# First V products and early gathers of a BigBird attention feeding a mixture of experts: who writes which half of the columns, and in what order the queues run

## The chip, the cores and the metric

One core of one Trainium2 chip runs the whole program: four batches of block-sparse attention, then a dropless mixture of experts on the attention's output. The metric is the device time of one execution in microseconds (us), as the median of several executions of the same program. The kernel before takes 633.23 us (three runs, 632.06 to 638.4).

## The reference, cut to what matters

```python
# attention: B, H, S, D = 4, 8, 768, 64; blocks of 32 rows, 24 of them
scores = scale * q @ k.T
mask = |block_i - block_j| <= 1, or either is the first or last block,
       or block_j is one of 3 sampled blocks of block_i
attn = exp(scores, masked) / (sum + 1e-9)
x = (attn @ v) as rows of B*S = 3072 tokens by H*D = 512
# mixture of experts: 8 experts, F = 1024
logits = x @ w_gate; e = argmax; gate = softmax(logits)[e]
y = gate * (relu(x @ w1[e]) @ w2[e])
```

All of it is float32. The first and the last 32 queries of a batch see every key; every other query sees a few blocks.

## The kernel before, in words

**Steps.** Attention runs in 48 steps, twelve to a batch: six groups of 128 queries, the last group first (`order`, line 98), and each group in two halves (`half` 0 and 1) of two head pairs. Steps are numbered 0 to 47 here; a batch's steps are 0 to 11, 12 to 23, 24 to 35, 36 to 47. The group that comes first in each batch (GL = 5) differs: 64 of its queries are ordinary, and the other 64 are the batch's first and last 32 rows, which see all 768 keys.

**Software pipeline.** In step i TensorE makes the scores of step i (`scores_near`, `scores_drawn`; `scores_all`, `scores_two` for the first group), ScalarE makes their exponentials (line 322), VectorE multiplies by the mask (lines 361, 396), and then TensorE makes the V products of step i - 1 (`attend`, `attend_last`; the matmul is line 416). VectorE divides them by their sums (`divide`, lines 483 to 489) and SP stores the rows in HBM (line 495). In batch 0 the products of the 64 queries that see all keys are made before step 0 for all four head pairs (`attend_all`, called in a loop behind `scores_first`).

**Column halves.** A V product is 128 keys by 64 queries times 128 by 65: it uses 64 of TensorE's 128 columns. `product` (line 412) writes rows 0 to 63 of a PSUM bank for `ti` 0 and rows 64 to 127 for `ti` 1. In the ordinary groups `ti` alternates from one product to the next. In the first group the ordinary 64 queries are `ti` 0 and the 64 that see all keys are `ti` 1: six products against twelve for each head pair, so six of the twelve stand alone, and in batch 0 all are made one half after the other.

**What feeds a step.** K and Q of the next batch come as eight pieces (n = 0 to 7: even K, odd Q, one for each head pair); SP loads each by two DMAs of 192 KB in 256-byte runs (`fill_stage`, line 143), and in steps 2, 4, 6 and 8 of a batch TensorE transposes two pieces (`turn`, line 181). V of the next batch is loaded and written out as rows of 2080 bytes (lines 164, 173). For a group's sampled blocks GpSimd gathers V rows by four indirect DMAs (`fetch_values`, line 568): (ti, ch) = (0,0), (1,0), (0,1), (1,1); products of the first chunk need neither, of the second chunk ch 0, of the third ch 1. A one-element copy (`not_before`, line 582) holds GpSimd's queue until a named piece of work is done. Keys of sampled blocks are copied by VectorE and ScalarE (`place_keys`, line 627), queries by VectorE (`place_queries`, line 609).

**Queues.** The order on TensorE, VectorE, GpSimd, ScalarE and SP is as the program is written. SP's queue holds the loads of K, Q and V, the stores of V rows and of the attention's rows, and in the last batch the expert weights: whatever waits there holds up all behind it. Pieces of the routing's layout (`early`, mostly VectorE) stand in half-0 steps.

**After attention** TensorE takes tiles of tokens through two layers (lines 1199 and 1213), with weights streamed ahead; the first tiles' rows are gathered (line 1117) in steps 45 to 47.

Of the kernel before, what the change touches and what calls it, by code (L numbers as in the profile page):

```python
# [17 lines left out]
def kernel(  # L18
# [367 lines left out]
    def scores_two(b, half):  # L386

        s, par = scored(), parity(b, GL)
        for i in range(2):
            pr = 2 * half + i  # L390
            to = s[:, i, : 6 * D].rearrange("p (h c q) -> p h c q", h=2, c=3)
            for ch, keys in enumerate([xk[:, par, pr, :]] + [kr[:, par, 0, pr, P * j : P * (j + 1)] for j in range(2)]):
                chunk_products(to[:, :, ch, :], keys, qz[:, pr, 0])
        e = exps(s, 6 * P * (3 * half + 2), 6 * D)
        both = e.rearrange("p i (h c q) -> p (i h) c q", h=2, c=3)
        nc.vector.tensor_tensor(both, both, mask[:, GL, :, 0, :].unsqueeze(1).to_broadcast([P, 4, 3, D]), op=ALU.mult)

        def at(i, hh, ch):
            x = (3 * hh + ch) * D
            return e[:, i, x : x + D]  # L400

        return at, e
# [9 lines left out]

    def product(b, g, pr, ti, hh, e, values, last):
        bank, begun = bank_of(b, g, pr)
        op = bank[:, : 4 * (D + 4)].rearrange("p (r h w) -> p r h w", r=2, h=2)
        nc.tensor.matmul(  # L416
            op[ti * D : (ti + 1) * D, pr % 2, hh, : D + 1], lhsT=e, rhs=values[:, (2 * pr + hh) * VW : (2 * pr + hh + 1) * VW],
            start=ti not in begun, stop=last, skip_group_check=True,
        )
        begun.add(ti)  # L420
# [9 lines left out]
    def attend_all(b, pr, e, chunks):  # L430
        for c in chunks:
            for hh in range(2):
                product(b, GL, pr, 1, hh, e(hh, c), sets[b][2][:, c, :], c == NCH - 1)

    def attend_last(b, pr, e_all, e_two):
        for ch in range(3):
            for hh in range(2):
                product(b, GL, pr, 0, hh, e_two(pr % 2, hh, ch), values_of(b, GL, 0, ch), ch == 2)
                if e_all is not None:
                    product(b, GL, pr, 1, hh, e_all(hh, ch), sets[b][2][:, ch, :], False)  # L440
        if e_all is not None:
            attend_all(b, pr, e_all, range(3, NCH))
# [29 lines left out]
    for pr in range(NPR):  # L472
        attend_all(0, pr, es[pr], range(NCH))
# [5 lines left out]
    def divide(b, g, half):  # L479
# [13 lines left out]
        if half == 1:  # L493
            for p, n, row in pieces(g):
                nc.sync.dma_start(x_d[b * S + row : b * S + row + n, :DM], xb[p : p + n, :])
# [31 lines left out]
    def logits(b, g, beside=None):  # L527
# [5 lines left out]
        for c in range(DB):  # L533
            for j in range(2):
                nc.tensor.matmul(
                    lg[j * D : (j + 1) * D, :], lhsT=xo[:, c * P + j * D : c * P + (j + 1) * D], rhs=wg[:, c, :],
# [848 lines left out]
    for i, (b, g, half) in enumerate(steps):  # L1385
# [15 lines left out]
        if two:  # L1401
# [4 lines left out]
            fetch_values(b_, g_, 0, 1)  # L1406
        if half == 1 and i + 1 < len(steps):
            place_queries(*steps[i + 1][:2], 0)
# [26 lines left out]
        if half == 1 and i + 1 < len(steps):  # L1435
            not_before(e[0:1, 0, 0:1])
            fetch_values(*steps[i + 1][:2], int(two), 1)
# [13 lines left out]
        if i > 0 and before[0][1] != GL:  # L1451
            attend(before)
        elif i > 0:
            for b_, g_, pr, e_all, at in before:
                attend_last(b_, pr, e_all, at)
# [6 lines left out]
        if i > 0:  # L1462
            divide(*steps[i - 1])
        early(late)
        if half == 0 and nxt is not None:
# [3 lines left out]
            if i >= 2 and len(tiles_of(nxt[1])) > 1:  # L1469
                b_, g_, half_ = steps[i - 1]  # L1470
                not_before(sums[0:1, b_ * NG + g_, 4 * half_ : 4 * half_ + 1])
                fetch_values(*nxt[:2], 1, 0)
        if half == 1 and nxt is not None:
# [189 lines left out]
```

## Time and profile before

| what | us |
|---|---|
| median of three runs | 633.23 (632.06 to 638.4) |
| the profiled execution, its own time | 632.67 |
| its span, first to last instruction | 631.0 |
| TensorE matmuls busy | 603.7 |
| VectorE, ScalarE, GpSimd busy | 329.6, 231.3, 188.1 |
| last V product of attention starts | 274.2 |

The page of the profile gives for each engine the busy time; the timeline gives merged instructions in order of time with the idle time before them and what ended it; the windows give busy time, granted TensorE clock (1.00 is full speed) and DMA load in a stretch. A float32 matmul stands in the trace as two records, so 48 products are 96 records. Matmul records overlap: how fast they follow each other is read from starts, not from their length. SPq and POOLq are the issuing sequencers.

### The profile page before, as it was taken

What the parts mean: (1) busy time and instruction counts of PE and PEld (TensorE: products, weight loads), DVE (VectorE), ACT (ScalarE), POOL (GpSimd) and SP (SyncE); (2) the same over time, 40 slices, a digit from 0 to 9 for tenths busy, and PEclk for the clock granted to TensorE, in tenths of its full rate; (3) what the DMA queues carried; (4) which work ended last, traced back from release to release, by engine and by line L of the source; (5) the groups of instructions that cost most, each with busy time, mean ns of one, the idle gap of its engine ahead of it and who ended that gap; (6) DMA issues with size and microseconds to landing.
All of it is one profiled execution on the core that took longest, in us unless ns stands there. A gap on an engine that the chain in (4) does not pass through costs nothing. (4 is left out here: it accounts for less than half of the span.)

```text
span 631.0 us, 19698 instructions
## 1 busy us (share of the span) xinstructions
PE 603.7 (96%) x8038; PEld 516.1 (82%) x8038; DVE 329.6 (52%) x1134; ACT 231.3 (37%) x447; POOL 188.1 (30%) x267
## 2 busy tenths in 40 slices
PE   6989999999998999999999999999999999999994
PEld 6888989998988998987777776877977787967862
DVE  7558876885688759726952494303190208203300
ACT  6457756775775668621111011111111111111110
POOL 2247853553355437610111211011401140020110
PEclk9879999999999999999999999999999999999998
DMA  8899977986895658799989999779998999779710
GB/s 267 209 183 256 249 197 181 247 234 168 180 220 178 206 161 262 270 334 378 324 305 328 341 391 344 274 251 377 397 400 304 370 398 399 270 228 407 284 41 20
DMA packets 125060, 170.83 MB, mean 271 GB/s; under 512 B 71236, under 2 KB 71237, under 8 KB 124934
## 3 DMA queue, kind: packets, MB, share of 16 engines
q1 hardware_dynamic: 114896, 137.61, 67.1%
q0 software_dynamic: 10000, 31.59, 15.9%
q8 instruction: 73, 1.20, 0.8%
q14 instruction: 53, 0.43, 0.2%
q10 hardware_dynamic: 38, 0.00, 0.0%
HBM read 150.11 MB, written 19.33 MB: 269 GB/s over the span
## 5 line engine op out<-in xcount | busy, mean ns | idle before, releaser
L568 POOL DMA_INDIRECT around<-v_rows,rows_of x88 | 103.4, 1175 | 94.8 <-PE op L416 45.6
L322 ACT ACTIVATE ea<-s 128x1024 f32<-128x1024 f32 (+1 forms) x84 | 81.3, 969 | 58.3 <-PE s L332 41.4
L1180 DVE STREAM_TRANSPOSE around<-xg 32x128 f32<-32x128 f32 x192 | 58.1, 303 | 84.9 <-DMA xg<-x_rows,gB 79.9
L1199 PEld LDWEIGHTS hp<-around,room 128*128 128x128 f32 x832 | 94.5, 192 | 2.9 <-issue 2.7
L1199 PE MATMUL hp<-around,room 128*128 128x128 f32 x832 | 96.2, 276 | 0.0
L332 PE MATMUL s<-room,kr 128*64 128x128 f32 x1408 | 91.3, 279 | 2.7 <-DVE room L609 2.7
L416 PE MATMUL op<-around,ea 128*64 128x65 f32 x2112 | 82.9, 223 | 10.2 <-DMA around<-v_rows,rows_of 9.3
L416 PEld LDWEIGHTS op<-around,ea 128*64 128x64 f32 x2112 | 78.4, 138 | 12.6 <-DMA around<-v_rows,rows_of 10.8
L332 PEld LDWEIGHTS s<-room,kr 128*64 128x64 f32 x1408 | 80.2, 139 | 5.1 <-ACT xo L512 2.8
L1213 PE MATMUL zp<-room,kr 128*128 128x512 f32 x176 | 77.6, 594 | 0.0
L1206 ACT ACTIVATE kr<-hp 128x512 f32<-128x512 f32 x36 | 21.5, 597 | 114.4 <-PE hp L1199 103.4
L1213 PEld LDWEIGHTS zp<-room,kr 128*128 128x128 f32 x176 | 32.6, 190 | 37.2 <-issue 37.0
L1233 POOL DMA_INDIRECT out_dram<-kr,sB x14 | 14.1, 1006 | 159.1 <-ACT kr L1223 98.0
L361 DVE TENSOR_TENSOR ea<-ea,mask 128x1024 f32<-128x1024 f32 x40 | 49.3, 1234 | 11.9 <-ACT ea L322 11.0
L1199 PEld LDWEIGHTS hp<-around,other 128*128 128x128 f32 x384 | 43.8, 192 | 2.3 <-issue 2.3
L1199 PE MATMUL hp<-around,other 128*128 128x128 f32 x384 | 44.3, 275 | 0.0
L1311 DVE STREAM_TRANSPOSE ea<-ea 32x128 f32<-32x128 f32 x84 | 21.7, 285 | 31.2 <-DMA ea<-x_rows,gB 30.6
L1223 ACT ACTIVATE kr<-zp,xg 128x512 f32<-128x512 f32 x12 | 8.2, 688 | 75.7 <-PE zp L1213 75.7
L1213 PE MATMUL zp<-other,kr 128*128 128x512 f32 x80 | 35.3, 594 | 0.0
L1180 DVE STREAM_TRANSPOSE around<-kr 32x128 f32<-32x128 f32 x48 | 14.5, 303 | 36.7 <-DMA kr<-x_rows,gB 35.3
L1213 PEld LDWEIGHTS zp<-other,kr 128*128 128x128 f32 x80 | 14.9, 190 | 17.4 <-issue 17.4
L1233 POOL DMA_INDIRECT out_dram<-kr,sA x5 | 5.1, 1021 | 73.5 <-ACT kr L1223 73.5
(380 smaller groups left out, 839.0 us busy)
## 6 DMA issues: line engine op xcount, KB each, us to landing
room<-in_moe_w_dram SPq DMA_DIRECT2D x30, 2048.0 KB
other<-in_moe_w_dram SPq DMA_DIRECT2D x16, 2048.0 KB
room<-in_moe_w_dram SPq DMA_DIRECT2D x16, 512.0 KB
x_rows<-xb SPq DMA_DIRECT2D x20, 256.0 KB
room<-in_k_dram SPq DMA_DIRECT2D x24, 192.0 KB
room<-in_q_dram SPq DMA_DIRECT2D x24, 192.0 KB
v_rows<-room SPq DMA_DIRECT2D x12, 260.0 KB
v_rows<-other SPq DMA_DIRECT2D x12, 260.0 KB
```

What stands on the lines that cost most here:

```text
L322: nc.scalar.activation(e, s[:, :, :n], AF.Exp, scale=scale)
L332: nc.tensor.matmul(to[j * D : (j + 1) * D], lhsT=keys[:, j * D : (j + 1) * D], rhs=queries, start=True, stop=True)
L361: nc.vector.tensor_tensor(both, both, m[:, None, :].to_broadcast([P, 4, 4 * D]), op=ALU.mult)
L416: nc.tensor.matmul(op[ti * D : (ti + 1) * D, pr % 2, hh, : D + 1], lhsT=e, rhs=values[:, (2 * pr + hh) * VW : (2 * pr + hh + 1) * VW], sta ...
L568: nc.gpsimd.indirect_dma_start(out=around[p0:, par, 1 + ti + 2 * ch, :], out_offset=None, in_=v_d[b][:, :], in_offset=bass.IndirectOffsetO ...
L1180: nc.vector.transpose(xT[d, :, t], xg[t, :DM].rearrange("p (c q) -> p c q", c=DB)[:, :, d])
L1199: nc.tensor.matmul(hp[:, m, :], lhsT=st[i]["w1"][:, c, fb * P : (fb + 1) * P], rhs=st[i]["xT"][:, c, :], start=(c == 0), stop=(c == DB - 1),)
L1206: nc.scalar.activation(hT[:, g * (FB // 2) : (g + 1) * (FB // 2), :], hp[:], AF.Relu)
L1213: nc.tensor.matmul(zp[:], lhsT=st[i]["hT"][:, fb, :], rhs=st[i]["w2"][:, fb, :], start=(fb == 0), stop=(fb == FB - 1),)
L1223: nc.scalar.activation(zo, zp[:], AF.Copy, scale=of_i)
L1233: ins = nc.gpsimd.indirect_dma_start(out=to[:, :], out_offset=bass.IndirectOffsetOnAxis(ap=at, axis=0), in_=rows, in_offset=None, bounds_c ...
L1311: nc.vector.transpose(xT_u[d, :, j * P + tq * 32 : j * P + (tq + 1) * 32], xg_u[t, j, :DM].rearrange("p (c q) -> p c q", c=DB)[:, :, d],)
```

## The change

It has four parts, all in the attention.

1. **Column halves.** A new `side_of` gives, for the first group only, the opposite halves to the odd head pairs: the all-keys products of pair 0 write rows 64 to 127, those of pair 1 rows 0 to 63. `in_turns` issues products of the two sides alternately: in batch 0 the all-keys products of pairs 0 and 1, then 2 and 3; in the other batches all-keys products first and the ordinary ones behind them. Since odd pairs' rows now lie swapped, the first group's store is six DMAs in 512-byte runs instead of three in 2048-byte runs, and `logits` takes the swapped half.
2. **First V products of batch 0.** The ordinary products of step 0 move from step 1 into step 2, beside those of step 1; their divisions follow there. Batch 0's exponentials in `scores_two` go to other places of the buffer (`half + 4`).
3. **Gathers and queries' copies.** `place_queries` for the next group's first half moves from the start of a half-1 step to the end of the half-0 step before it, directly behind `divide`. The gather (0,1) follows it there, held by a `not_before` on those queries; (1,1) moves up to the start of the half-1 step, behind the `not_before` on the copied keys; the `not_before` on the masked exponentials is gone.
4. **Layout pieces** (`early`) come one step later, in half-1 steps, behind the gathers' issue.

```diff
-        e = exps(s, 6 * P * (3 * half + 2), 6 * D)
+        e = exps(s, 6 * P * (3 * half + 2 if b > 0 else half + 4), 6 * D)
...
+    def side_of(g, pr, ti):
+        return (ti + pr) % 2 if g == GL else ti
+
     def product(b, g, pr, ti, hh, e, values, last):
         bank, begun = bank_of(b, g, pr)
+        side = side_of(g, pr, ti)
...
-            op[ti * D : (ti + 1) * D, pr % 2, hh, : D + 1], lhsT=e, rhs=values[:, (2 * pr + hh) * VW : (2 * pr + hh + 1) * VW],
-            start=ti not in begun, stop=last, skip_group_check=True,
+            op[side * D : (side + 1) * D, pr % 2, hh, : D + 1], lhsT=e, rhs=values[:, (2 * pr + hh) * VW : (2 * pr + hh + 1) * VW],
+            start=side not in begun, stop=last, skip_group_check=True,
...
+    def of_all(b, pr, e):
+        return [(b, GL, pr, 1, hh, e(hh, c), sets[b][2][:, c, :], c == NCH - 1) for c in range(NCH) for hh in range(2)]
+
+    def of_last(b, pr, e):
+        return [(b, GL, pr, 0, hh, e(pr % 2, hh, ch), values_of(b, GL, 0, ch), ch == 2) for ch in range(3) for hh in range(2)]
+
+    def in_turns(*sides):
+        for two in zip(*sides, strict=True):
+            for one in two:
+                product(*one)
+
+    def attend_first(prs):
+        in_turns(*(of_all(0, pr, es[pr]) for pr in prs))
+
+    def attend_last(units_):
+        sides = [[], []]
+        for b, _, pr, e_all, _ in units_:
+            if e_all is not None:
+                sides[1 - pr % 2] += of_all(b, pr, e_all)
+        for b, _, pr, _, at in units_:
+            sides[pr % 2] += of_last(b, pr, at)
+        in_turns(*sides)
...
-    for pr in range(NPR):
-        attend_all(0, pr, es[pr], range(NCH))
+    for half in range(2):
+        attend_first((2 * half, 2 * half + 1))
...
+                for a in range(2):
+                    for p, n, row in pieces(g):
+                        p = (p + a * D) % P
+                        nc.sync.dma_start(
+                            x_d[b * S + row : b * S + row + n, :DM].rearrange("n (r a w) -> n r a w", r=2, a=2)[:, :, a],
+                            xb[p : p + n, :].rearrange("n (r a w) -> n r a w", r=2, a=2)[:, :, a],
+                        )
...
             if i == 1:
                 fetch_values(b_, g_, 1, 0)
-            fetch_values(b_, g_, 0, 1)
-        if half == 1 and i + 1 < len(steps):
-            place_queries(*steps[i + 1][:2], 0)
+            fetch_values(b_, g_, 1, 1)
...
-        if half == 1 and i + 1 < len(steps):
-            not_before(e[0:1, 0, 0:1])
-            fetch_values(*steps[i + 1][:2], int(two), 1)
...
-        if i > 0 and before[0][1] != GL:
+        if i == 1:
+            begun = before
+        elif i > 0 and before[0][1] != GL:
             attend(before)
         elif i > 0:
-            for b_, g_, pr, e_all, at in before:
-                attend_last(b_, pr, e_all, at)
+            for units in ([begun] if i == 2 else []) + [before]:
+                attend_last(units)
...
-        if i > 0:
+        if i == 2:
+            divide(*steps[0])
+        if i > 1:
             divide(*steps[i - 1])
-        early(late)
...
                 fetch_values(*nxt[:2], 1, 0)
+            place_queries(*nxt[:2], 0)
+            not_before(qz[0:1, 0, 0, 0, 0:1])
+            fetch_values(*nxt[:2], 0, 1)
+        early(late - 1)
```

How it moves the instructions, at three places. Names: `op` is the products' bank, `s` the scores, `tp` transposed K and Q, `xk` and `kr` keys, `around` gathered V rows, `ea` the exponentials, `room` and `other` the two big buffers that hold K, Q and V (`room` also the copied queries).

First, TensorE in batch 0, from the end of step 1's scores (first row) through steps 2 and 3. Before:

```order
L332 MATMUL s<-room,kr 64x2x64 x4
L416 MATMUL op<-around,ea 64x65 x12
L181 MATMUL tp<-ident,room 128x64 x24
L340 MATMUL s<-room,xk 128x128 x8
L332 MATMUL s<-room,kr 64x2x64 x16
L416 MATMUL op<-around,ea 64x65 x12
L332 MATMUL s<-room,kr 64x2x64 x16
L416 MATMUL op<-around,ea 64x65 x24
```

With the change:

```order
L332 MATMUL s<-room,kr 64x2x64 x4
L181 MATMUL tp<-ident,room 128x64 x24
L340 MATMUL s<-room,xk 128x128 x8
L332 MATMUL s<-room,kr 64x2x64 x16
L420 MATMUL op<-around,ea 64x65 x24
L332 MATMUL s<-room,kr 64x2x64 x16
L420 MATMUL op<-around,ea 64x65 x24
```

The twelve ordinary products of step 0 no longer stand between the scores of step 1 and step 2's transposes of K and Q pieces 0 and 1; those follow the scores at once, and the twelve stand with step 1's twelve.

Second, GpSimd through steps 4 and 5: the four gathers for step 6's group, in the order (0,0), (1,0), (0,1), (1,1), with the one-element copies that hold the queue and pieces of the routing's constants between. Before:

```order
L568 DMA around<-v_rows,rows_of 64x520
L582 COPY paced<-sums 1x1
L568 DMA around<-v_rows,rows_of 64x520
L753 IOTA kx_i 1x31
L755 CAST kx<-kx_i 1x31
L753 IOTA eid_i 1x8
L755 CAST eid<-eid_i 1x8
L582 COPY paced<-kr 1x1
L568 DMA around<-v_rows,rows_of 128x520
L582 COPY paced<-ea 1x1
L568 DMA around<-v_rows,rows_of 128x520
```

With the change:

```order
L591 DMA around<-v_rows,rows_of 64x520
L605 COPY paced<-sums 1x1
L591 DMA around<-v_rows,rows_of 64x520
L605 COPY paced<-room 1x1
L591 DMA around<-v_rows,rows_of 128x520
L776 IOTA kx_i 1x31
L778 CAST kx<-kx_i 1x31
L776 IOTA eid_i 1x8
L778 CAST eid<-eid_i 1x8
L605 COPY paced<-kr 1x1
L591 DMA around<-v_rows,rows_of 128x520
```

The third gather moves ahead of the constants and of the wait for keys (it waits for the queries now, `paced<-room`), and the fourth takes over that wait and loses the one for the exponentials.

Third, VectorE from the division in step 32. Before, the layout piece (`offA` to `slA`) follows it; behind that come, in step 33, the copied keys, and only then the queries of step 34 (line 609) and the mask of step 33:

```order
L483 TENSOR_SCALAR sums<-op 128x4
L485 RECIPROCAL r<-sums 128x4
L489 TENSOR_TENSOR xb<-op,r 128x256
L918 SCALAR_TENSOR_TENSOR offA<-loA,cnA 128x8
L919 TENSOR_SCALAR offA<-offA 128x8
L878 TENSOR_TENSOR slot<-rA,offA 128x96
L884 TENSOR_TENSOR slot<-slot,selA 128x96
L885 TENSOR_REDUCE slA<-slot 128x12
```

With the change the queries (line 632) follow that division at once, ahead of the copied keys, which begin with the load of their indices:

```order
L496 TENSOR_SCALAR sums<-op 128x4
L498 RECIPROCAL r<-sums 128x4
L502 TENSOR_TENSOR xb<-op,r 128x256
L632 COPY room<-room 64x4x64 x2
L645 TENSOR_LOAD from_k
```

and the layout piece stands behind the mask and the division of step 33:

```order
L361 TENSOR_TENSOR ea<-ea,mask 128x1024
L496 TENSOR_SCALAR sums<-op 128x4
L498 RECIPROCAL r<-sums 128x4
L502 TENSOR_TENSOR xb<-op,r 128x256
L941 SCALAR_TENSOR_TENSOR offA<-loA,cnA 128x8
L942 TENSOR_SCALAR offA<-offA 128x8
L901 TENSOR_TENSOR slot<-rA,offA 128x96
L907 TENSOR_TENSOR slot<-slot,selA 128x96
L908 TENSOR_REDUCE slA<-slot 128x12
```

So the queries have moved ahead of the layout piece and the keys, and the piece has moved back by a step.

On SP the first group's six stores (32 or 64 rows by 2 by 128) stand where three stood, in steps 2, 14, 26 and 38, ahead of the next loads of V and of K and Q pieces.

More of the change, by code (lines that the diff above doesn't have):

```diff
@@ L411, in bank_of @@
         return banks_of[key]
+    def side_of(g, pr, ti):
+        return (ti + pr) % 2 if g == GL else ti
     def product(b, g, pr, ti, hh, e, values, last):
         bank, begun = bank_of(b, g, pr)
+        side = side_of(g, pr, ti)
         op = bank[:, : 4 * (D + 4)].rearrange("p (r h w) -> p r h w", r=2, h=2)
         nc.tensor.matmul(
-            op[ti * D : (ti + 1) * D, pr % 2, hh, : D + 1], lhsT=e, rhs=values[:, (2 * pr + hh) * VW : (2 * pr + hh + 1) * VW],
-            start=ti not in begun, stop=last, skip_group_check=True,
+            op[side * D : (side + 1) * D, pr % 2, hh, : D + 1], lhsT=e, rhs=values[:, (2 * pr + hh) * VW : (2 * pr + hh + 1) * VW],
+            start=side not in begun, stop=last, skip_group_check=True,
         )
-        begun.add(ti)
+        begun.add(side)
     def attend(units_):
@@ L428, in attend @@
                         product(b, g, pr, ti, hh, e(pr % 2, hh, ti, ch), values_of(b, g, ti, ch), ch == 2)
[L430 to L442, printed above, removed]
+    def of_all(b, pr, e):
[16 more added lines that the diff above has]
+        in_turns(*sides)
     def turn_first(pr):
@@ L493, in divide @@
         if half == 1:
-            for p, n, row in pieces(g):
-                nc.sync.dma_start(x_d[b * S + row : b * S + row + n, :DM], xb[p : p + n, :])
+            if g < GL:
+                for p, n, row in pieces(g):
+                    nc.sync.dma_start(x_d[b * S + row : b * S + row + n, :DM], xb[p : p + n, :])
+            else:
+                for a in range(2):
+                    for p, n, row in pieces(g):
+                        p = (p + a * D) % P
[3 more added lines that the diff above has]
+                        )
     def pieces(g):
@@ L534, in logits @@
             for j in range(2):
+                from_ = side_of(g, c, j)
                 nc.tensor.matmul(
-                    lg[j * D : (j + 1) * D, :], lhsT=xo[:, c * P + j * D : c * P + (j + 1) * D], rhs=wg[:, c, :],
+                    lg[j * D : (j + 1) * D, :], lhsT=xo[:, c * P + from_ * D : c * P + (from_ + 1) * D], rhs=wg[:, c, :],
                     start=(c == 0), stop=(c == DB - 1), skip_group_check=True,
```

## The prediction

> **What bounds the kernel now.** I read the page first, then TensorE's waits, then windows, then the timelines of TensorE, SP, GpSimd and VectorE around each wait.
>
> ```profile
> PE 603.7 (96%) x8038; PEld 516.1 (82%) x8038; DVE 329.6 (52%) x1134; ACT 231.3 (37%) x447; POOL 188.1 (30%) x267
> ```
>
> ```profile
> PE op L416 <- DMA around<-v_rows,rows_of: 9.3, 11, 1.9
> PE s L332 <- DVE room L609: 2.7, 3, 1.7
> PE op L416 <- DVE ea L396: 0.7, 1, 0.7
> ```
>
> ```profile
> 32.50:39.30 6.80, 6.09 (x64) 5.75 (x66) 3.38 (x12) 2.14 (x5) 2.40 (x4) 0.50 1.20 234
> 39.30:203.10 163.80, 155.55 (x3652) 151.20 (x3649) 124.94 (x426) 111.49 (x212) 87.56 (x135) 1.00 0.84 207
> 203.20:206.50 3.30, 3.30 (x34) 3.30 (x34) 3.14 (x10) 0.00 (x0) 3.13 (x3) 0.50 0.89 277
> 300.00:631.00 331.00, 322.21 (x2094) 247.03 (x2093) 115.83 (x397) 48.13 (x90) 51.15 (x52) 0.99 0.84 307
> ```
>
> TensorE bounds it: 603.7 of 631.0 us. Second rows: in the attention it waits 9.3 us for gathers, 2.7 us for copied queries, 0.7 us for a mask. Windows (TensorE busy first, then loads, VectorE, ScalarE, GpSimd, clock, DMA load): the clock falls to 0.50 after two of these waits, and half speed over 6.8 and 3.4 us is 3.4 and 1.7 us lost. From 39.3 on the other engines keep TensorE over 94% busy. The experts behind 300 us are untouched.
>
> **Part 1, first V products and step 2.** Two products on the same columns follow each other; two on opposite halves share a slot.
>
> ```profile
> 20.34 2.72 PE L416 MATMUL op<-room,ea 128*64 128x65 f32 x26
> 23.23 4.12 PE L416 MATMUL op<-room,ea 128*64 128x65 f32 x67 [0.17 <-issue]
> 30.85 0.45 PE L416 MATMUL op<-around,ea 128*64 128x65 f32 x4 [0.70 <-DVE ea L396]
> 33.21 2.43 PE L416 MATMUL op<-around,ea 128*64 128x65 f32 x20 [1.91 <-DMA around<-v_rows,rows_of]
> 35.57 1.55 PE L181 MATMUL tp<-ident,room 64*128 64x64 f32 x24
> 40.86 1.50 PE L416 MATMUL op<-around,ea 128*64 128x65 f32 x23
> 43.95 1.62 PE L416 MATMUL op<-around,ea 128*64 128x65 f32 x48
> ```
>
> Single: 67 records in 4.12 us, less the last one's 0.22, are 58 ns each. Alternating: 48 records in 1.62 less 0.22 are 58 ns a pair. So the all-keys products, 20.34 to about 27.1, end some 3 us sooner, the two steps' scores behind them (3 us in the old trace) end near 27, and without step 0's products TensorE stands at step 2's transposes near 27 instead of 35.57. It would be 7 to 8 us ahead. But those transposes need K piece 0 and Q piece 1:
>
> ```profile
> 26.80 0.99 SPq L143 DMA_DIRECT2D room<-in_k_dram  x2
> 27.83 2.40 SPq L143 DMA_DIRECT2D room<-in_q_dram  x2
> 44.14 1.64 SPq L495 DMA_DIRECT2D x_rows<-xb  x3
> 46.37 1.17 SPq L143 DMA_DIRECT2D room<-in_q_dram  x2
> 55.59 3.48 SPq L143 DMA_DIRECT2D room<-in_q_dram  x2
> ```
>
> ```profile
> 27.32 0.93 POOL L568 DMA_INDIRECT around<-v_rows,rows_of  x1 [0.30 <-issue]
> ```
>
> The gather issued at 27.32 ended TensorE's wait at 33.21: 5.9 us in that crowded stretch. With 5.9 us the second Q DMA (begun near 28.4 to 29, issue ended 30.23) lands between 34.3 and 36.1; the old trace bounds it too, since the Q half of the 24 transposes ran near 36.2 without a wait. I take 35.6. SP's loads at 26.8 wait for nothing that the change moves. So the 7 to 8 us turn into a wait for Q, and the half clock of 32.5 to 39.3 stays. Behind it the same scores follow, and the 24 ordinary products of steps 0 and 1, now 24 pair slots, take what step 1's 24 single records took at 40.86. Gain: the K transposes done early, about 0.6 us, less 0.3 because two gathers come sooner and share the DMA: **0.3 us**, bounds -1 (one more gather lands in front of Q) and +7 (Q lands by 29). The exponentials' new places cost nothing: ScalarE no longer waits there for the all-keys products to be read, and whatever it does sooner or later by a microsecond lies under the wait for Q.
>
> **Part 2, six stores on SP.** Three stores take 1.64 us of SP, so three more 1.6; the second division is about 0.3 later. SP's next loads come 1.9 us later, Q piece 7 with them: its issue ended at 59.07, with 5.9 us it lands at 65.0, and it is transposed in the second of these rows:
>
> ```profile
> 64.99 0.59 PE L181 MATMUL tp<-ident,room 64*128 64x64 f32 x12
> 65.54 0.54 PE L181 MATMUL tp<-ident,room 64*128 64x64 f32 x12
> ```
>
> The slack is about 0.5 us. With 1.9 us of delay, and TensorE a microsecond earlier (part 3), step 8 waits about **1.9 us** (bounds 0, if SP catches up while it has nothing to issue, and 3). Batch 1 has the same order with more slack; I take 0.4 there, nothing in batch 2; batch 3 loads no K or Q after its stores.
>
> **Part 3, gathers.** Group 1's gathers and the products that wait for the last of them:
>
> ```profile
> 44.50 0.94 POOL L568 DMA_INDIRECT around<-v_rows,rows_of  x1 [0.16 <-issue]
> 45.98 1.96 POOL L568 DMA_INDIRECT around<-v_rows,rows_of  x1 [0.35 <-PE op L416]
> 48.48 0.98 POOL L568 DMA_INDIRECT around<-v_rows,rows_of  x1 [0.16 <-issue]
> ```
>
> ```profile
> 55.38 0.68 PE L416 MATMUL op<-around,ea 128*64 128x65 f32 x14 [1.17 <-DMA around<-v_rows,rows_of]
> 82.74 0.33 PE L416 MATMUL op<-around,ea 128*64 128x65 f32 x2 [0.61 <-DMA around<-v_rows,rows_of]
> 83.83 0.68 PE L416 MATMUL op<-around,ea 128*64 128x65 f32 x14 [0.76 <-DMA around<-v_rows,rows_of]
> ```
>
> The waits stand before the third chunk, the last 14 or 16 of 48 records. Its gathers went out at 45.98 and 48.48; with the change one follows the gather of 44.50 as soon as the queries are copied (VectorE, 0.6 us) and the other the keys' copy: about 1 to 2 us sooner each. The added wait for the queries holds the third gather, the constants behind it and the fourth, and behind these only TensorE's third chunk; it ends 0.6 us after the division, while GpSimd is still issuing the second gather. The waits besides the first (1.9) are 7.4 us in ten, at most 1.2 each, so a lead of 1 to 2 covers most. Batch 0: 2.5 us of them, of which I count 2.0 back. The others: 4.9, of which 4.5 back (the rest where transfers are crowded). With part 2 batch 0 nets 0.3 + 2.0 - 1.9 = **0.4**, and batches 1 to 3 net 4.5 - 0.4 = **4.1 us**. Bounds: 0 for the gathers if they only queue longer in the DMA engines, 7.4 if all goes.
>
> **Part 4, pairing in batches 1 to 3.**
>
> ```profile
> 94.61 0.22 PE L416 MATMUL op<-around,ea 128*64 128x65 f32 x1
> 94.61 0.22 PE L416 MATMUL op<-other,ea 128*64 128x65 f32 x1
> 95.26 0.75 PE L416 MATMUL op<-other,ea 128*64 128x65 f32 x10
> 96.54 1.04 PE L416 MATMUL op<-other,ea 128*64 128x65 f32 x15
> 97.51 0.59 PE L181 MATMUL tp<-ident,room 64*128 64x64 f32 x12
> ```
>
> From 94.61 to 97.51 a first-group step takes 2.90 us: alternating rows start together, but twelve products, 24 records, stand alone. Paired they fill 12 slots fewer: 12 x 58 = 0.7 us, two steps in three batches: 4.2. In the second step of each batch the logits already overlap the single tail, so **3.5 us** (bounds 0, below, and 4.2). TensorE is gapless there, so this shows in full.
>
> A rule of the Trainium skill speaks against it ("TensorE: Matmul & The Clock Gate", Part 3, The mechanism): weight loads overlap matmuls in flight only between different row groups; all these products use the same 128 rows, so alternate columns would gain nothing and the sum would be 3.5 us worse. The rows at 94.61 show otherwise.
>
> **Part 5, queries and layout pieces.**
>
> ```profile
> 199.17 0.42 DVE L489 TENSOR_TENSOR xb<-op,r 128x256 f32<-128x256 f32 x1
> 199.51 0.16 DVE L918 SCALAR_TENSOR_TENSOR offA<-loA,cnA 128x8 f32<-128x8 f32 x1
> 201.71 0.50 DVE L627 COPY kr<-room 128x128 f32 x3 [0.90 <-issue]
> 202.32 0.58 DVE L609 COPY room<-room 64x256 f32<-64x256 f32 x2
> ```
>
> ```profile
> 203.05 3.62 PE L332 MATMUL s<-room,kr 128*64 128x128 f32 x32 [1.73 <-DVE room L609]
> ```
>
> The queries that TensorE waits for until 203.05 are copied at 202.32, behind a layout piece and the keys; with the change they follow the division at 199.5. The copies take the same 0.6 us of VectorE; the keys now start that much later behind them, and end when they did. Of 2.7 us I count **2.1** back, since the piece, one step later, can delay keys or a mask instead, and the half clock behind 203.2, **1.7 us**. Bounds -1 and 4.4. The last piece leaves the first tile's gather where it was: it is issued behind group 4's last gather, which moves up as much as TensorE does; if it is late, the first experts' tile pays up to 1 us.
>
> **Sum**: 0.4 + 4.1 + 3.5 + 2.1 + 1.7 = 11.8 us off the profiled execution's 632.67 (span 631.0, so 1.7 lie around it), which is 0.6 under the median 633.23: 620.9, I say **621.0**.
>
> **Rivals.**
> - *Q is there in time*: the 7 us of part 1 come through: 614. For it: nothing but the possibility that Q's landing is earlier than its use shows; against it the 5.9 us. Chance 0.10.
> - *DMA and SP give it back*: gathers that start sooner share the engines with K and Q, whose pieces land later; half of the 4.5 us is not returned, and steps 8 and 20 wait 3.3 us more in sum: 621 + 2.2 + 3.3 = 626.5, 624 to 629. For it: DMA load 1.20 in the window at 32.5; against it 0.84 on the mean from 39.3. Chance 0.20.
> - *Alternate columns of the new order don't overlap*: part 4 is 0: 624.5. Chance 0.05.
> - *Slower*: SP behind the stores. These three stores of a few bytes took 3.30 us, 1.1 each:
>
> ```profile
> 110.64 3.30 SPq L562 DMA_DIRECT2D x_rows<-gw  x3
> ```
>
> If six short-run stores cost 1.1 each, SP is 5 us late, K and Q of batches 1, 2 and 3 miss their step by 3 to 4.5 us, about 12 in all, and each such wait halves the clock, 1.7 each: 621 + 12 + 5 = 638. It decides from about 4 us of delay on. Against it 1.64 for three such stores now. Chance 0.05.
> - The forecast has 0.58; the last 0.02 are without a cause that I can name.
>
> The Trainium skill ("TensorE: Matmul & The Clock Gate", Part 1) has the clock halved after one idle window of about 3.4 us; by that a wait of 2 us for Q piece 7 costs no clock. In this trace 1.73 us was enough, so I allow for one more dip.
>
> **How the numbers follow.** A measurement of this kernel can tell about 1%, 6.3 us. Faster by more: 0.58 + 0.10 + 0.05 + half of 0.20 = 0.83; within: the other half and the rest, 0.12; slower 0.05. Forecast alone: 617 to 625. Range: 613.5, to hold the first rival, to 629, to hold the second.
>
> **What would show it.** Step 2's transposes wait near 27 to 35.6 and the products behind them end near 42, as before: part 1 right; if they end near 35, wrong. First-group steps of 2.1 us instead of 2.9: part 4. Waits on gathers of about 1 us in sum instead of 9.3 and none at 203: parts 3 and 5. A new wait of about 2 us at step 8's transposes: part 2. I am wrong if products still wait for gathers, or if SP stands at the first group's stores for over 4 us.

## The result, and the profile after

The changed kernel takes 640.46 us (median of 4, 638.98 to 641.48) where the kernel before takes 632.64 (median of 4): 1.0108 of it, 95% interval 1.0063 to 1.0153. It is slower by 7.8 us; 621.0 was forecast. The profiled execution took 640.52, its span is 638.7.

The page's first part, for the change:

```profile
PE 600.4 (94%) x8038; PEld 512.4 (80%) x8038; DVE 328.5 (51%) x1134; ACT 231.6 (36%) x447; POOL 189.5 (30%) x267
```

TensorE's busy time fell by 3.3 us, and yet the span grew by 7.7. TensorE's waits in the change (sum, times, longest):

```profile
PE tp L181 <- DMA room<-in_q_dram: 9.2, 4, 3.3
PE op L420 <- DMA around<-v_rows,rows_of: 7.1, 6, 3.0
PE tp L181 <- DMA room<-in_k_dram: 4.2, 1, 4.2
PE s L340 <- DVE cnA L868: 1.7, 1, 1.7
PE s L332 <- DVE tvA L1090: 0.7, 1, 0.7
PE s L332 <- DVE room L632: 0.5, 1, 0.5
```

The wait for queries is down from 2.7 to 0.5 us as meant, but the gathers still cost 7.1 of 9.3, and 9.2 us for pieces of Q, 4.2 for one of K and 2.4 for layout pieces are new. The 4.2 for K and 2.1 of those for Q stand at the start, where part 1 had them: the products behind them end at 42.6, against 42.4 before. TensorE's timeline of the change, at these waits and at a first-group step:

```profile
32.77 0.59 PE L181 MATMUL tp<-ident,room 64*128 64x64 f32 x12 [4.17 <-DMA room<-in_k_dram]
35.43 0.91 PE L181 MATMUL tp<-ident,room 64*128 64x64 f32 x12 [2.07 <-DMA room<-in_q_dram]
41.07 1.56 PE L420 MATMUL op<-around,ea 128*64 128x65 f32 x48
...
69.47 0.59 PE L181 MATMUL tp<-ident,room 64*128 64x64 f32 x12 [3.27 <-DMA room<-in_q_dram]
...
88.71 1.13 PE L420 MATMUL op<-around,ea 128*64 128x65 f32 x14 [2.36 <-DMA around<-v_rows,rows_of]
...
102.48 1.57 PE L420 MATMUL op<-other,ea 128*64 128x65 f32 x48
103.89 0.86 PE L420 MATMUL op<-around,ea 128*64 128x65 f32 x24
104.68 0.59 PE L181 MATMUL tp<-ident,room 64*128 64x64 f32 x12
...
136.71 0.91 PE L181 MATMUL tp<-ident,room 64*128 64x64 f32 x12 [2.76 <-DMA room<-in_q_dram]
...
190.64 2.02 PE L340 MATMUL s<-room,xk 64*128 64x128 f32 x16 [1.70 <-DVE cnA L868]
```

The start went as forecast (Q's wait ends at 35.43, the products behind it at 42.6). A first-group step takes 2.20 us, from 102.48 to 104.68, against 2.90. But the transposes of Q piece 7 wait 3.27 us in step 8 (69.47) and 2.76 in step 20 (136.71). SP's timeline of the change shows why:

```profile
45.14 4.21 SPq L514 DMA_DIRECT2D x_rows<-xb  x6
...
49.94 1.16 SPq L143 DMA_DIRECT2D room<-in_q_dram  x2
51.15 3.27 SPq L164 DMA_DIRECT2D other<-in_v_dram  x2
54.52 2.78 SPq L143 DMA_DIRECT2D room<-in_k_dram  x2
...
60.94 3.83 SPq L143 DMA_DIRECT2D room<-in_q_dram  x2
```

Six stores took 4.21 us, 0.70 each, not 3.2. Q piece 5 left at 49.94 instead of 46.37 (3.6 late: the stores began 1.0 later and took 2.6 longer) and piece 7 at 60.94 instead of 55.59 (5.35 late): SP had no pause in which to catch up, and the loads behind the stores took longer too.

The time from step 2's near scores (line 340) to the first expert matmul can be split. The waits are the idle times over 0.05 us before TensorE's matmuls; "half clock" is half the time at granted clock 0.50; "own" is the rest. All in us, from one timeline each; the kernels e5 to e18 come below (in e15 and e18 the stretch begins 7 to 8 us earlier in time, and holds two pieces' transposes more).

| kernel | total | waits | half clock | own |
|---|---|---|---|---|
| before | 237.4 | 10.4 | 2.9 | 224.2 |
| before, another execution (e5) | 238.8 | 13.2 | 1.7 | 223.9 |
| change | 246.1 | 17.9 | 9.1 | 219.1 |
| change, another execution (e6) | 239.8 | 13.7 | 6.4 | 219.6 |
| three stores (e7) | 235.6 | 12.0 | 3.8 | 219.9 |
| three stores made six, runs of 1 KB (e9) | 242.2 | 14.0 | 9.2 | 219.0 |
| twelve stores (e12) | 241.1 | 16.8 | 5.1 | 219.3 |
| pairing alone, three stores (e8) | 237.4 | 13.1 | 5.0 | 219.4 |
| old gathers (e11) | 235.0 | 12.9 | 1.9 | 220.2 |
| transposes behind scores (e15) | 235.1 | 11.7 | 1.7 | 221.7 |
| change, stores a step later (e17) | 237.6 | 10.8 | 7.4 | 219.4 |
| change, transposes behind scores (e18) | 244.8 | 17.3 | 6.8 | 220.7 |

So pairing took 4 to 5 us off TensorE's own time in every kernel that has it (2 to 4 in e15 and e18, whose stretch holds more). In the change, waits (+7.5) and half clock (+6.2) took more. One execution's waits vary by several us (the change: 17.9 and 13.7), so the verdicts below go by the timed runs.

### The profile page after: what moved, and what is told of

Its sections match the earlier page's. It is cut to its first block, busy times and chain, and to the rows that moved or that the text cites. A ratio compares the mean times of both kernels' runs of the same rounds, so it can differ in the third digit from the quotient of the medians.

```text
span 638.7 us, 19713 instructions
## 1 busy us (share of the span) xinstructions
PE 600.4 (94%) x8038; PEld 512.4 (80%) x8038; DVE 328.5 (51%) x1134; ACT 231.6 (36%) x447; POOL 189.5 (30%) x267
## 5 line engine op out<-in xcount | busy, mean ns | idle before, releaser
L591 POOL DMA_INDIRECT around<-v_rows,rows_of x88 | 105.6, 1200 | 125.2 <-PE op L420 74.3
L420 PE MATMUL op<-around,ea 128*64 128x65 f32 x2112 | 73.5, 222 | 7.7 <-DMA around<-v_rows,rows_of 7.1
L420 PEld LDWEIGHTS op<-around,ea 128*64 128x64 f32 x2112 | 69.8, 138 | 9.6 <-DMA around<-v_rows,rows_of 7.9
L181 PE MATMUL tp<-ident,room 64*128 64x64 f32 x288 | 14.1, 235 | 13.4 <-DMA room<-in_q_dram 9.2
```

Source lines behind the costliest of these rows:

```text
L181: nc.tensor.transpose(tp[:, j, c * D : (c + 1) * D], src[r, c, :], ident[r, r])
L420: nc.tensor.matmul(op[side * D : (side + 1) * D, pr % 2, hh, : D + 1], lhsT=e, rhs=values[:, (2 * pr + hh) * VW : (2 * pr + hh + 1) * VW], ...
L591: nc.gpsimd.indirect_dma_start(out=around[p0:, par, 1 + ti + 2 * ch, :], out_offset=None, in_=v_d[b][:, :], in_offset=bass.IndirectOffsetO ...
```

## The experiments

Times stand as a ratio to the kernel before on the same device, with its 95% interval; 0.01 is 6.3 us. The runs fell on four devices: e1 to e4, e5 to e8, e9 to e16, and e17 and e18.

**e1 to e4: the first separation, spoiled.** e1 is before with the column halves, six stores and logits of the change, all else at its old place. e2 is the change with the old sides and three stores. e3 writes the odd pairs' halves back in the division:

```diff
+parts = [(0, 0, P, slice(0, 4))] if g < GL else [(0, 0, P, slice(0, 2)), (0, D, D, slice(2, 4)), (D, 0, D, slice(2, 4))]
+for p, f, n, c in parts:
+    nc.vector.tensor_tensor(to[p : p + n, c], op[f : f + n, c, :D], r[f : f + n, c]...)
```

e4 issues the six stores in the next step (3 of a batch), behind its loads:

```diff
-            else:
-                for a in range(2): ...            # in divide, step 2
+        if i > 2 and half == 1 and steps[i - 3][1] == GL and here == 3:
+            leave_rows(b, GL)                     # behind fill_next of step 3
```

> The kernel before with the column halves alone: alternate sides by pair of heads in the first groups' products, six stores for a first group, the logits' halves turned; step 0's products, the gathers, the queries and the layout pieces stay where they were. Theory S (the six stores hold SP for 4.3 us against 1.6, and the K and Q behind them reach their steps late): the pairing wins about 3.5 us in batches 1 to 3 and 3 at the start, of which the Q wait at step 2 takes most back, and SP's delay costs 3 to 4 us in each of three batches and one or two half-clock stretches: about 638, 635 to 641, with waits on a Q or K piece at steps 6 to 8 and 18 to 20. Theory M (the moved gathers, queries and layout pieces are the loss): this kernel has none of them and is at 629, 627 to 631, with no wait on Q or K between 45 and 260 us.

> The change without the column halves: step 0's products in step 2, gathers, queries' copies and layout pieces at their new places, but the old sides and three whole-row stores. Theory S: no loss by SP, the gathers' and queries' waits fall: about 626, 622 to 630. Theory M: the moves themselves cost: about 640 or above (the change, 640, plus the 3 us that the pairing would have won): 638 to 645, with the waits of the change at 88, 190 and 260 us.

> The whole change, but the division writes the odd pairs' halves back to their rows (three VectorE multiplications of the first group's division instead of one), so three whole-row stores do and the logits read as before. Theory S: SP is as early as before, the Q waits at steps 8 and 20 (3.3 and 2.8 us) and their half clock go: about 630, 626 to 633. Theory M: the waits on gathers and on the layout piece stay and with them the time: 637 to 641, whether or not SP is early.

> The whole change with its six stores, issued one step later, behind the next step's loads of K, Q and V, so that these no longer stand behind them. Theory S: Q piece 5 and K piece 6 leave SP 4 us sooner; Q piece 7 still follows the stores, so the wait at step 8 shrinks but need not vanish: 630 to 636. Theory M: 637 to 641.

Measured: e1 643.88, 1.0086 [1.0055, 1.0116]; e2 654.71, 1.0263 [1.0234, 1.0292]; e3 656.38, 1.0268 [1.0238, 1.0297]; e4 660.86, 1.0356 [1.0315, 1.0398]; before 638.4 there. By the times theory M wins by far. The timelines say otherwise. In e1, which has the six stores, the transposes of steps 6 and 8 wait for Q (0.86 us at 57.89, 1.67 at 69.20), as theory S has it, though none does in steps 18 to 20. In e2, e3 and e4 no transposes wait for K or Q behind 40 us, as theory S has it too. What e3 has instead stands in TensorE's timeline, and in its waits (second piece):

```profile
130.32 0.25 PE L420 MATMUL op<-around,ea 128*64 128x65 f32 x1 [0.16 <-issue]
131.06 0.25 PE L420 MATMUL op<-around,ea 128*64 128x65 f32 x1 [0.49 <-issue]
```

```profile
PE op L420 <- issue: 13.5, 23, 2.5
```

One record, later up to six, every 0.74 us, and nothing that the profile names is waited for, until the step ends. Such stretches come about once in 10 us (two steps) in e2, e3 and e4, fewer and shorter in e1. The traces of before and of the change have none. So these four times tell nothing of the theories until the stretches are explained.

**e5 to e8: the same on another device.** e5 is before, e6 the change, e7 the kernel of e3, all unchanged. e8 is before with pairing and the division of e3 (three stores), no moves.

> The kernel before, unchanged, for its own trace beside the next three. The last three kernels' traces show something that neither the trace of before nor that of the change has: stretches in which TensorE issues two to ten products every 0.74 us and waits for nothing that the profile names (12 to 18 us in sum in the kernels with the moved gathers, 4 us in the one without). Theory D (it belongs to the device that ran them, whatever the kernel): on that device this trace has 5 us of it or more and about 638; on another none and about 633. Theory O (it belongs to the order of the instructions): none here, 633 to 638.

> The change, unchanged. Theory D: on the device of the runs before, 12 us or more in such stretches and 650 to 660; on another none and 640. Theory O: as in its first trace none, 640, with the waits on the Q pieces at 69 and 137 us.

> The change with the odd pairs' halves written back by the division and three whole-row stores, as run before at 656. Theory D: if this device shows the stretches in e6, 656 again; if not, 627 to 633, since its first trace had no wait on a Q piece at steps 8 and 20. Theory O: 656 with the stretches, whatever e6 shows.

> The kernel before with the pairing alone, written back by the division, with three whole-row stores: no move of step 0's products, gathers, queries or layout pieces. Theory S (the six stores on SP are the loss, the pairing itself wins): 3.5 us in batches 1 to 3 and up to 3 at the start, less what the wait for the second step's Q piece takes back: 3 to 6 us under the kernel before. Theory P (alternate columns win nothing here): as before, within 1 us. Theory M (the moves lose): also 3 to 6 under, and then e7 without the stretches must still be slower than this one by 5 us or more.

Measured: e5 1.0001 [0.9958, 1.0043]; e6 637.24, 1.0091 [1.0059, 1.0123]; e7 631.08, 0.9988 [0.996, 1.0016]; e8 634.29, 1.0001 [0.9961, 1.0041]. None of the four shows the stretches, and the kernel of e3 is 1 us under before instead of 18 over, in ratio 0.9988 against 1.0268: the stretches come with the device (seen on one, at one time), as theory D has it. Three stores instead of six are worth 0.0103, **6.5 us**, and that is nearly the whole loss. Theory M falls: with all moves and three stores the kernel is not slower. But it is not 14 us faster either, as the forecast without its stores would be, and pairing alone (e8) wins nothing that can be told. That is the time of theory P, but not its cause: TensorE's own time falls by 4.5 us in e8 (table). TensorE's waits for gathers in e5 and in e8:

```profile
PE op L416 <- DMA around<-v_rows,rows_of: 8.1, 9, 1.8
```

```profile
PE op L420 <- DMA around<-v_rows,rows_of: 12.4, 13, 3.8
```

Of these 4.3 us more, 3.8 are one wait at the start (34.16), which TensorE reaches sooner. In the table's stretch the waits are as long as in e5 (13.1 and 13.2), and 3.3 us more at half clock take most of the 4.5.

The traces of e6 and e7 don't show the 6.5 us as late pieces: in e6's, Q piece 7 leaves SP at 58.40, sooner than e7's (60.70), and is in time, while a gather of step 6 is 1.38 us late at 65.88. Why that gather is late isn't shown.

**e9 and e12: the number of stores.** e9 is e7 with each store as two halves of 256 columns. e12 is the change with a store for each head pair, twelve in all, in the same 512-byte runs.

```diff
-for a in range(2):                               # e12
+for pr in range(NPR):
     for p, n, row in pieces(g):
-        p = (p + a * D) % P
+        p = (p + pr % 2 * D) % P
```

> The kernel of e7 (halves written back by the division), but each of the first group's three stores is two again, one for each half of the columns, so that six stores leave in runs of 1 KB. Theory I (the number of issues on SP): SP stands 4.3 us at them as in the change, and the time goes up to that of the change, 6 us over e7. Theory R (the change's short runs of 512 bytes, 1536 more packets, load the DMA engines): at most half of the packets are added, 1 to 2 us over e7 or nothing.

> The change with twelve stores for a first group instead of six, one for each pair of heads, in the same runs of 512 bytes, so as many packets as in the change. Theory I: SP stands 8 to 9 us at them, the K and Q behind leave 4 us later still, and all of that comes through, since in the change they are late already: 5 to 15 us over the change, 642 to 652. Theory R: as the change, within 2 us.

Measured: e9 636.83, 1.0063 [1.0019, 1.0107]; e12 638.19, 1.0124 [1.0044, 1.0204]. SP's first-group stores in e7, e9 and e12:

```profile
46.83 1.60 SPq L510 DMA_DIRECT2D x_rows<-xb  x3
```

```profile
45.19 3.84 SPq L512 DMA_DIRECT2D x_rows<-xb  x6
```

```profile
44.52 8.40 SPq L514 DMA_DIRECT2D x_rows<-xb  x12
```

```profile
PE tp L181 <- DMA room<-in_q_dram: 11.1, 6, 4.1
```

The last row is TensorE's wait for Q in e12 (1.8 in e7). From three stores to six the number of issues counts: 0.9988 and 1.0063. Six stores in runs of 1 KB already cost 0.0075 of the 0.0103; the other 0.0028 is inside the noise, so that short runs cost anything isn't shown. Twelve (1.0124) can't be told from six (1.0091): the 5 us or more of theory I didn't show, and theory R's time fits e12 as well. What theory I says of SP did come, 8.40 us at the stores and 11.1 us of waits for Q, but the gathers' waits are shorter there (3.4 us, 7.1 in the change).

**e10, e11, e13: what the moves are worth.** On e7: e10 puts the layout pieces back (`early(late)` behind the division), e11 the gathers, e13 both.

```diff
-            fetch_values(b_, g_, 1, 1)            # e11, e13
+            fetch_values(b_, g_, 0, 1)
...
+        if half == 1 and i + 1 < len(steps):
+            not_before(e[0:1, 0, 0:1])
+            fetch_values(*steps[i + 1][:2], int(two), 1)
```

> The kernel of e7 with the layout pieces back at their old place, one step earlier and ahead of the queries. Theory L (the moved pieces put waits of their own in place of those they remove: 1.6 us for the piece that holds a score bank at 186, 0.7 for the tokens at 263): these two waits go and nothing comes for them: 2 us under e7, up to 4 where the half clock behind the first goes too. Rival: the queries behind the pieces are late again as in before (1.7 us and its half clock at 203): 1 to 3 us over e7.

> The kernel of e7 with the gathers back at their old places (one behind the first key copies of the second half, one behind the exponentials); the queries' copies stay at the new place. Theory G (the earlier gathers win what the prediction counted, 6.5 us of waits): 637 or 6 over e7, gather waits of 10 us and more. Rival Q (the DMA engines are the limit where the waits are, and a gather that is issued sooner lands no sooner): within 2 us of e7, with the wait near 85 to 88 us as large.

> The kernel of e11 (halves written back, gathers at their old places) with the layout pieces back at their old place as well: of the moves only step 0's products and the queries' copies are left. Theory G2 (the moves of gathers and layout pieces win nothing that can be measured): as e11, 0.995 to 1.000 of the kernel before. Rival G (they won what was forecast and something else took it): 4 us or more over e11.

Measured: e10 632.1, 1.001 [0.9974, 1.0047]; e11 629.52, 0.9972 [0.9935, 1.0008]; e13 631.13, 0.999 [0.9966, 1.0015]. All the same as e7 within 0.3%. Theory G falls by 7 us, and the 2 us of theory L don't show: the moved gathers and the moved layout pieces are worth nothing that can be told, in either direction.

**e14, e15, e16: where the won time waits.** On e11: e14 loads K and Q pieces 0 and 1 of the batch after next two steps later; e15 turns step 2's two pieces behind that step's scores; e16 is both and e13's layout.

```diff
-if b + 1 < B and half == 0 and 2 <= here < 10:              # e15
+if b + 1 < B and half == 0 and 2 <= here < 10 and i > 2:
...
 at, e = scores_two(b, half) if g == GL else scores_drawn(b, g, half, near)
+if i == 2:
+    for n in range(2):
+        turn(1, 0, n, 0)
```

> The kernel of e11 with the loads of K and Q pieces 0 and 1 of the next batch but one issued in steps 10 and 11 of a batch, with pieces 2 and 3, instead of in steps 8 and 9. Theory DMA (in steps 8 to 10 every transfer lands 6 to 7 us after its issue because these loads, the stores of V rows and the gathers stand in one line, and TensorE's waits for gathers there come from that, not from when the gathers are issued): the waits on gathers from 78 to 100 us fall under 0.6 us, gathers issued there land within 4 to 5 us: 1 to 3 us under e11. Rival POOL (they come from when GpSimd issues): as e11, with the same waits.

> The kernel of e11 with the first two transposed pieces of the next batch, in step 2, behind that step's scores instead of ahead of them. Theory K (at the start the K and Q pieces set the end, and the pairing's gain there goes into waiting for them): the wait of 8 us before the transposes shrinks by the 3 us of scores that now come first, and the first products of steps 0 and 1 start that much sooner: 2 to 3 us under e11. Rival V (the gathers of steps 0 to 2 are as late as K and Q): the wait comes back before the products, within 1 us of e11.

> The edits of e13, e14 and e15 in one kernel. By the theories DMA and K the gains add: 4 to 6 us under e11, 0.988 to 0.992 of the kernel before. By their rivals: as e11.

Measured: e14 631.59, 0.998 [0.9947, 1.0014]; e15 **624.5, 0.989 [0.9858, 0.9922]**; e16 626.3, 0.9928 [0.9886, 0.997]. e15 is 5 us under e11 and 7 under before. TensorE's timeline of e15:

```profile
29.11 1.16 PE L340 MATMUL s<-room,xk 64*128 64x128 f32 x16
...
31.09 2.28 PE L332 MATMUL s<-room,kr 128*64 128x128 f32 x28 [0.20 <-DVE kr L646]
34.38 0.59 PE L181 MATMUL tp<-ident,room 64*128 64x64 f32 x12 [1.02 <-DMA room<-in_k_dram]
37.28 0.82 PE L181 MATMUL tp<-ident,room 64*128 64x64 f32 x12 [2.31 <-DMA room<-in_q_dram]
```

The scores now run at 29 to 33 while K and Q are under way; of the waits for K and Q 3.3 us are left, of 5.5 in e11:

```profile
32.04 0.59 PE L181 MATMUL tp<-ident,room 64*128 64x64 f32 x12 [2.86 <-DMA room<-in_k_dram]
35.28 0.90 PE L181 MATMUL tp<-ident,room 64*128 64x64 f32 x12 [2.66 <-DMA room<-in_q_dram]
```

That is the 2 to 3 us expected (step 4's transposes start at 44.01, in e11 at 46.10). The rest came later, and in these two executions the gathers' waits fell with no edit of theirs, from e11 to e15:

```profile
PE op L420 <- DMA around<-v_rows,rows_of: 8.5, 9, 1.8
```

```profile
PE op L420 <- DMA around<-v_rows,rows_of: 4.1, 6, 0.9
```

e14 tells against theory DMA: with two loads fewer the waits near 85 us are as in e11 (0.34 and 0.70 against 0.36 and 0.76). e14 won nothing, and e16 has nothing over e15.

**e17 and e18: SP's line by itself.** e17 is the kernel of e4; e18 the change with the edit of e15 and its six stores.

> The kernel of e4 again, on a device that does not show the starved stretches: the change with its six stores issued one step later, behind the next step's loads. Theory I (SP's line: what stands behind the stores is late): the stores cost SP as much as ever, but Q piece 5 and K piece 6 leave ahead of them, so half or more of the 6 us comes back: 631 to 634, 0.998 to 1.003 of the kernel before. Rival W (six stores cost what they cost in the DMA engines, wherever they stand): as the change, 1.007 to 1.011.

> The change as it is, six stores and all, with step 2's two transposed pieces behind that step's scores, as in e15. If the wait at the start and SP's line are two separate losses, the 5 us of e15 come here too: 631 to 633, 0.999 to 1.002. Rival: TensorE, 5 us earlier behind the start, reaches step 8 before its Q piece, which the six stores hold, and waits there for what it won: 636 or more.

Measured: e17 629.77, 0.9948 [0.9913, 0.9983]; e18 630.89, 0.9951 [0.9911, 0.9991]. In e17 the same six stores, 3.54 us of SP, stand one step later, and the loss is gone (1.0091 to 0.9948, 9 us). SP's timeline of e17, and TensorE's wait in step 8:

```profile
40.88 1.59 SPq L143 DMA_DIRECT2D room<-in_q_dram  x2
44.91 3.54 SPq L520 DMA_DIRECT2D x_rows<-xb  x6
...
54.90 4.43 SPq L143 DMA_DIRECT2D room<-in_q_dram  x2
```

```profile
65.81 0.59 PE L181 MATMUL tp<-ident,room 64*128 64x64 f32 x12 [0.51 <-DMA room<-in_q_dram]
```

Q piece 5 leaves 9 us sooner than in the change: neither behind the stores nor behind the division that they wait for. In before it stands behind that division too (46.37), so e17 also wins something that before doesn't have. K piece 6 does not leave ahead of the stores, as was expected, but behind them (50.38), 4 us sooner than in the change; Q piece 7 is 6 us sooner, and the wait of 3.27 us is 0.51. Rival W falls: it is not what the six stores are, but what stands behind them. So the times show the cause of the stores' loss: it comes with their number (e7, e9) and goes with their place (e17). That it runs through late pieces of Q, the traces of the change and of e12 show; what made e6 longer than e7 stays open.

e18 wins 9 us over the change where the 5 of e15 were expected. The noise allows both, but its trace shows that the two losses are not separate. SP's timeline of e18:

```profile
40.66 3.56 SPq L514 DMA_DIRECT2D x_rows<-xb  x6
...
53.86 3.51 SPq L143 DMA_DIRECT2D room<-in_q_dram  x2
```

The six stores stand where they stood, but the products that they wait for come 4.2 us sooner, the stores leave 4.5 us sooner (45.14 in the change), Q piece 7 leaves 7 us sooner (60.94), and TensorE, in step 8 at 62.0, doesn't wait for it. So an earlier start takes away part of the stores' loss as well; how much isn't shown. e17's place of the stores with e15's transposes wasn't tried.

## Why the prediction was wrong, by its own steps

- Forecast and time are 19.5 us apart. Part 2 is about 4 of them (6.5 lost for 2.3). The larger share is the gain of parts 3 to 5: by them e7, which has three stores, should be 14 us under before, and it is 1 under.
- **Part 1 (0.3 us): right**, its ends to within 0.6 us (TensorE began to wait at 28.6, not 27). More was to be had there: e15 takes 2 us at the start, and 5 in all, by not letting TensorE wait for a piece that it doesn't need yet.
- **Part 2 (a loss of 2.3 us): the step that failed first.** "SP's next loads come 1.9 us later": they came 3.6 later, and 5.35 by Q piece 7, since the stores began 1.0 us later (0.3 in the sum), six take 4.2 us, and SP behind them is never idle. The term cost 6.5 us (e6 against e7). The prediction's slower rival described this, with its point of decision at about 4 us of delay and 638 us; it was given 0.05 because three stores took 1.64. That its 638 came so near is in part luck: it had 12 us of waits for K and Q and 5 at half clock, where the change has 7.2 us of such waits behind the start and 6.8 at half clock, and the rest is gains that did not come. SP's timeline of before held the other half of the answer: between 44.14 and 59.07 it has no pause over 0.3 us, so a delay could only be handed on.
- **Part 3 (6.5 us back): failed.** The gathers' waits fell from 9.3 to 7.1 us (8.9 in e6). "About 1 to 2 us sooner each" holds for one of the two gathers, and the waits stand before the other. GpSimd and TensorE's near scores of step 10, before and in the change:

```profile
73.99 1.16 PE L340 MATMUL s<-room,xk 64*128 64x128 f32 x16
...
75.88 1.08 POOL L568 DMA_INDIRECT around<-v_rows,rows_of  x1 [0.15 <-DVE r L485]
76.96 0.32 POOL L582 COPY paced<-ea 1x1 f32<-1x1 f32 x1
77.44 0.99 POOL L568 DMA_INDIRECT around<-v_rows,rows_of  x1 [0.16 <-PE s L332]
```

```profile
77.98 1.16 PE L340 MATMUL s<-room,xk 64*128 64x128 f32 x16
...
77.87 2.04 POOL L591 DMA_INDIRECT around<-v_rows,rows_of  x1 [0.16 <-issue]
80.97 0.29 POOL L605 COPY paced<-kr 1x1 f32<-1x1 f32 x1
81.52 1.08 POOL L591 DMA_INDIRECT around<-v_rows,rows_of  x1 [0.26 <-PE s L332]
```

  Against the scores, the third gather went from 1.89 us behind to 0.11 ahead, the fourth from 3.45 behind to 3.54 behind. It gained nothing here, but not for want of keys, of which VectorE finishes its share at 77.42:

```profile
77.13 0.29 DVE L654 COPY kr<-room 128x256 f32<-128x256 f32 x1
```

  It is GpSimd's own line: from the first gather to the fourth it takes 7.1 us before (70.32 to 77.44) and 7.3 in the change (74.24 to 81.52), with no pause over 0.3 us. The constants that stood ahead of the third gather now stand ahead of the fourth (79.92 to 81.0), and the third took 2.04 us instead of 1.08. What sets the rest of these waits stays open: e11 (old places), e14 (fewer loads) and e15 (another phase) speak against the issue alone and against those loads.
- **Part 4 (3.5 us): right on TensorE** (2.20 for 2.90 us a step; own time down by 4 to 5), **wrong on the path**: "TensorE is gapless there, so this shows in full". It was gapless in those steps, but the gathers and pieces that come next are not paced by TensorE, and TensorE met them sooner: in e8 a wait of 3.8 us for a gather at the start, and 3.3 us more at half clock behind it, took what pairing won.
- **Part 5 (2.1 and 1.7 us): mis-sized to nothing.** The wait for queries went, and the layout pieces put 1.70 (190.64) and 0.7 us in its place, where "since the piece, one step later, can delay keys or a mask instead" had allowed 0.6; the half clock moved from behind 203.2 to behind 190.7. VectorE's row of the change that ends the wait:

```profile
190.42 0.17 DVE L868 COPY cnA<-layA 128x16 f32<-128x16 f32 x1
```

  The piece is short, but until it runs it holds one of three score banks, and it now stands behind a mask and a division.
- The clock: one more dip was allowed for, though the sum has no term for it. Three began at these waits, at 88.34 (two windows long), 136.13 and 190.74: 6.8 us lost, against 1.7 before.
- The Trainium skill's rule that weight loads overlap matmuls in flight only between different row groups ("TensorE: Matmul & The Clock Gate", Part 3, The mechanism) did not hold here. From 102.48 to 104.68 weight loads are busy 2.13 of 2.20 us beside matmuls, all products on the same 128 rows, and the products on alternate columns overlap. Their gain in the sum was rightly taken from the rows.

## What to carry to other kernels

A layout that is free for the engine that computes may cost issues on a queue: count what stands behind those issues and whether that queue has a pause to catch up in, and if not, put the stores behind the next loads. Time won on the engine that bounds is kept only as far as what it meets next is early enough; look for the first thing that it waits for without needing it, and move that. For a gather issued sooner, look at the last one that its consumer needs, and at what the issuing queue itself has to do before it.

## What the runs showed of the hardware

**When the clock halves.** Windows of the change (length, TensorE busy first, clock behind the engines):

```profile
64.45:67.86 3.41, 1.76 (x54) 1.55 (x50) 3.17 (x10) 2.48 (x6) 3.23 (x5) 1.00 0.96 191
67.86:71.27 3.41, 1.80 (x36) 1.71 (x38) 1.58 (x7) 1.05 (x3) 1.96 (x5) 1.00 1.12 283
71.27:74.69 3.42, 3.42 (x96) 3.42 (x94) 1.10 (x3) 2.57 (x7) 0.45 (x1) 1.00 0.37 118
...
187.33:190.74 3.41, 1.71 (x48) 1.48 (x44) 3.17 (x12) 2.23 (x5) 3.07 (x4) 1.00 0.77 162
190.74:194.15 3.41, 3.41 (x32) 3.19 (x33) 2.19 (x9) 1.02 (x1) 1.04 (x1) 0.50 1.15 300
```

The dips here begin on a grid of 3.413 us (88.34 to 190.74 is 30 times that, to 136.13 14 times). The wait of 3.27 us at 69.47 lies across two windows, TensorE is busy 1.76 and 1.80 us in them, and the clock stays; the wait of 1.70 at 190.64 lies in one, TensorE is busy 1.71 us, and the next window runs at half speed. So a wait costs about double when it falls inside one such window. Over the 1236 windows from 20 to 300 us of before, the change and e5 to e18, run at full clock, the next ran at half speed behind all 29 with TensorE busy under 1.53 us and behind none with over 1.71; of the 12 between, 7 fell. The limit is near half a window of work, but the busy time alone doesn't settle it: on the device of e1 to e4, where the products came singly, it fell behind up to 2.30 us. The Trainium skill ("TensorE: Matmul & The Clock Gate", Part 1, What's actually happening) has the free-running window of 3413 ns, which agrees, but asks for an idle window of about 3.4 us; these rows show that about half of one idle was enough.

**Starved TensorE.** On the device of e1 to e4 TensorE got its products a few at a time every 0.74 us, 13.5 us in sum at the products of e3 alone, and the same two kernels that took 1.0268 and 1.0356 of before there took 0.9988 and 0.9948 elsewhere. The kernel before lost less (638.4 against 632). Why it comes, and why to some orders of instructions more than to others, the runs don't show.
